# Long convolution and soft MoE on one core: a start without clearings, loads in two bursts per pair of steps, and the signal load split into 64 and 32 rows

## The chip, the core and the metric

The kernel runs on one core of a Trainium2 chip. The metric is the device time in microseconds (us) of one execution, the median of several runs. The engines are PE (TensorE matmul; PEld is its weight load), DVE (VectorE), ACT (ScalarE), POOL (GpSimd) and SP (SyncE, which here only issues DMA transfers). All of them work on their own instruction streams and meet through semaphores.

## The reference

A causal convolution of eight sequences of 5696 tokens and 128 channels with a filter as long as the sequence, and a soft mixture of experts over all 45568 tokens of its output:

```python
# x (8, 5696, 128), h (5696, 128); L = 2 * 5696
y = irfft(rfft(x, L, axis=1) * rfft(h, L, axis=0), L, axis=1)[:, :5696]
x = y.reshape(45568, 128)
logits = x @ phi                         # phi (128, 32): 8 experts, 4 slots each
d = exp(logits - logits.max(0));  d /= d.sum(0) + 1e-9      # over tokens
slot_input = d.T @ x
slot_out[e] = relu(slot_input[e] @ w1[e]) @ w2[e]           # 128 -> 1024 -> 128
c = exp(logits - logits.max(1));  c /= c.sum(1) + 1e-9      # over slots
return c @ slot_out
```

Everything is float32.

## The kernel before

The convolution is done as a transform in two stages, of 90 and 64 points, forward and back, all as matmuls with tables that are loaded from DRAM. Three stages follow each other with a lag, and their intermediates go through DRAM.

- **Stage A** (`stage_a`): the first forward stage. Columns of a sequence are loaded in chunks. `load_x(m)` (line 178) loads one pair of chunks into a tile `xc` of 128 partitions, 4 KB on either side of the sequence to a row; there are two such tiles. The filter `h` has 89 rows and comes as two blocks of 80 and 9 rows; a batch of `x` comes as one block of 96 rows (`XR`). `fold(c)` (209) on POOL adds and subtracts the two sides into one of three tiles `x`; the matmuls at 241 contract all 128 partitions of it. ACT evicts the result into `fst` (243), and SP writes it to DRAM as `f`, low rows (60) in every step, high rows (30) of two chunks in every odd step.
- **Stage B**: `load_g` (264) reads a tile `gt` of `f` (512 KB, 3 buffers). `stage_b1` (275) multiplies by the table `wt` (matmuls at 284) and by the filter's spectrum on DVE (304, 312). For the filter itself (g = 0) it makes that spectrum, `Hr` and `Hi`. `stage_b2` (316) goes back with the table `vt` (327), ACT evicts to `zst` (332), and SP writes `zm` (the first 64 rows) or `zr` (the rest).
- **Stage C**: `load_main` and `load_rest` read `zc` and `zx`, `stage_c1` finishes the transform (412, 417), and c2 to c6 transpose, form logits, both softmaxes, and gather the slots' input. `c_t` keeps the weights in DRAM for the tail, in which the experts and the output are computed.

The steps t = 0, 1, ... of the main loop (631) are written out by hand. A step runs stage A of chunk t, the units of stage B of eight and more steps before, and stage C of a lag of 27 steps. Eight steps (NJ) are one sequence, the filter first and then eight batches; a sequence has 12 units of stage B, one in an odd step and two in an even one. Stage A ends at step 72.

The order in the code is the order on each engine. SP alone issues nearly all transfers, so its instruction order is a queue, too: a transfer that waits holds all behind it. `pending` collects writes, and `flush()` issues them. `prefetch(last)` issues the `gt` loads up to a unit, but none before step 8g + 8 for a sequence g; it is called by `slot_b`, just after `stage_b1` of a unit, so that a load follows each unit (`AHEAD` is 3). In an even step the order of issue is: `load_rest` (only where a batch's first pair needs it), `load_x`, `flush()` of the low `f` writes, and then `gt` after the first unit, writes, `gt` after the second. In an odd step: `flush()`, `load_main`, `load_rest`, `gt`, writes.

Ahead of the loop (615 to 627) SP issues the first two loads of the filter and the tables `wt` and `vt`. ACT issues the other tables and then eight transfers that clear the part of `zr` that stage B never writes; their source is the tile `zx`, cleared by a memset at 359. Memsets at 175 clear the two `xc` tiles, for the rows that no load fills.

Of the kernel before, what the change touches and what calls it, by code (L numbers as in the profile page):

```python
# [70 lines left out]
def kernel(  # L71
# [24 lines left out]
    nc = tc.nc  # L96
    P = 128
# [5 lines left out]
    N1, N2 = 90, 64  # L103
    R1, HALF, NP = S // N2, N2 // 2, N1 // 2
    CH = 4
    NJ = HALF // CH
# [6 lines left out]
    NQ = NJ // 2  # L113
    assert S == R1 * N2 and R1 == N1 - 1 and D == P and CH == Q == 4
    LOW, MAIN = 60, HP
    XR = -(-R1 // 16) * 16
    ctx.enter_context(tc.manual_schedule())

    t_s1, t_im, t_ir, t_w, t_v, t_turn = [
        nc.inline_tensor(t, f"tab_{n}").ap()  # L120
        for n, t in zip(("s1", "im", "ir", "w", "v", "turn"),
                        transform_tables(S, N1, N2, CH, LOW, MAIN, XR))]
# [38 lines left out]
    wt = fconst.tile([P, NP, HP], F32, name="wt")  # L161
    vt = fconst.tile([P, NU, 2, HP], F32, name="vt")
# [9 lines left out]
    xs = {}  # L172
    xf = [apool.tile([P, 2, CH, D], F32, name=f"x{i}", tag=f"x{i}", bufs=1) for i in range(3)]
    xcs = [apool.tile([P, 2, 2 * CH, D], F32, name=f"xc{i}", tag=f"xc{i}", bufs=1) for i in range(2)]
    for t_ in xcs:
        nc.vector.memset(t_[:, :, :, :], 0.0)

    def load_x(m, halves=((0, 2 * CH),)):

        if 2 * m >= (B + 1) * NJ:  # L180
            return
        g, j = divmod(2 * m, NJ)
        if g == 0:
            src, blocks = h, ((0, R1 // 16 * 16), (R1 // 16 * 16, R1))
        else:
            r0 = min((g - 1) * R1, B * R1 - XR) * N2
            src, blocks = x.rearrange("b t d -> (b t) d")[r0:r0 + XR * N2], ((0, XR),)
        src = src.rearrange("(a n) d -> a n d", n=N2)
        t_ = xcs[m % len(xcs)]
        for n0, n in halves:  # L190
            a = (CH * j + n0, N2 - CH * j - n0 - n)
            p = (n0, 2 * CH - n0 - n)
            for r0, r1 in blocks:
                if n == 2 * CH:
                    v = src[r0:r1, a[0]:a[0] + n, :]
                    v = bass.AP(tensor=v.tensor, offset=v.offset,
                                ap=[v.ap[0], [(a[1] - a[0]) * D, 2], [1, n * D]])
                    nc.sync.dma_start(
                        out=t_[r0:r1, :, :, :].rearrange("p s n d -> p s (n d)"), in_=v)
                    continue  # L200
                for s_ in range(2):
                    nc.sync.dma_start(
                        out=t_[r0:r1, s_, p[s_]:p[s_] + n, :].rearrange("p n d -> p (n d)"),
                        in_=src[r0:r1, a[s_]:a[s_] + n, :].rearrange("r n d -> r (n d)"))
        xs[2 * m] = xs[2 * m + 1] = t_

# [2 lines left out]
    def fold(c):  # L209
        if c not in xs:  # L210
            return
        t_ = xs.pop(c)
        y_ = xf[c % len(xf)]
        i = CH * (c % 2)
        near, far = t_[:, 0, i:i + CH, :], t_[:, 1, ::-1, :][:, i:i + CH, :]
        for o in range(2):
            nc.gpsimd.tensor_tensor(out=y_[:, o, :, :], in0=near, in1=far,  # L217
                                    op=AL.subtract if o else AL.add)
        folded[c] = y_

# [2 lines left out]
    def flush():  # L223
        while pending:
            pending.pop(0)()
# [153 lines left out]
    def load_rest(T):  # L379
        if T >= NT:  # L380
            return
        b, j = divmod(T, NQ)
        t_ = zs[T]
        n = 2 * CH
        nc.sync.dma_start(
            out=t_[1][:, :, :, :].rearrange("p h n d -> p (h n d)"),
            in_=zr[(b + 1) % 2].rearrange("o c k r d -> (o c k) r d")[:, j * n:(j + 1) * n].rearrange(
                "p r x -> p (r x)"))
# [212 lines left out]
    NA, NC = (B + 1) * NJ, B * NJ  # L601
# [10 lines left out]
    AHEAD = 3  # L612
# [2 lines left out]
    load_x(0, ((0, CH), (CH, CH)))  # L615
    nc.scalar.dma_start(out=s1[:, :, :, :], in_=t_s1)
    load_x(1)
    nc.sync.dma_start(out=wt[:, :, :], in_=t_w)
    nc.sync.dma_start(out=vt[:, :, :, :], in_=t_v)
    nc.scalar.dma_start(out=phi[:, :], in_=moe_phi)  # L620
    nc.scalar.dma_start(out=turn[:, :, :, :, :], in_=t_turn)
    nc.scalar.dma_start(out=im[:, :, :], in_=t_im)
    nc.scalar.dma_start(out=ir[:, :], in_=t_ir)
    for i in range(8):
        nc.scalar.dma_start(
            out=zr[i // 4][i // 2 % 2, i % 2, N1 - MAIN:].rearrange("k (j r) d -> (k j) (r d)", r=2 * CH),
            in_=zring[0][1][0:4 * (HALF - N1 + MAIN), :, :, :].rearrange("p h n d -> p (h n d)"))
    fold(0)
    wait_b2 = []

    for t in range(last_front + 1):
        us = list(units(t))

        def pair(lag):
            T, half = divmod(t - LAG_C - lag, 2)
            return T if half == 0 and 0 <= T < NT else None

        def prefetch(last):
            nonlocal loaded
            while loaded < len(queue) and queue[loaded][0] <= last \  # L640
                    and queue[loaded][0] // NW * NJ + NJ <= t:
                load_g(queue[loaded][0])
                loaded += 1

        def slot_b(due=True):
            fresh = due and bool(us)
            if fresh:
                u = us.pop(0)
                stage_b1(u)
                prefetch(u + AHEAD)  # L650
                wait_b2.append(u)
            if len(wait_b2) > fresh:
                stage_b2(wait_b2.pop(0))

        T, U, V, W, X = [pair(k) for k in (0, 2, 1, 3, 5)]
        if t < NA:
            stage_a(t, False)
            fold(t + 1)
        if t == last_front:
            assert T is None and U is None  # L660
            assert pair(-1) % NQ
            flush()
            dispatch(W)
            for i in range(3):
                slot_b()
                flush()
                if i == 1:
                    softmax_sum(W)
                    stage_c2(V)
            assert not us and not wait_b2  # L670
            stage_c6(X)
            stage_c3(V)
            column_max(V)
            break
        if t % 2:
            if T is not None:
                stage_c1(T)()
            flush()
            if pair(-2) is not None:
                load_main(pair(-2))  # L680
                if pair(-2) % NQ:
                    load_rest(pair(-2))
            slot_b()
            if U is not None:
                stage_c4(U)
            if t < NA:
                stage_a(t, True)
            if U is not None:
                stage_c5(U)
                softmax_exp(U)  # L690
            flush()
        else:
            if pair(-1) is not None and pair(-1) % NQ == 0:
                load_rest(pair(-1))
            if t < NA:
                load_x(t // 2 + 2)
            flush()
            if t == NJ:
                prefetch(AHEAD - 1)
            slot_b()  # L700
            if W is not None:
                softmax_sum(W)
                dispatch(W)
            flush()
            if V is not None:
                stage_c2(V)
            if X is not None:
                stage_c6(X)
            slot_b()
            if V is not None:  # L710
                stage_c3(V)
                column_max(V)
            flush()
        if t == NA:
            lead.close()
            wts = inner.enter_context(tc.tile_pool(name="wts", bufs=1, side="right"))
            w1s = wts.tile([P, E, F], F32, name="w1s")
        if NA < t <= NA + E:
            nc.sync.dma_start(out=w1s[:, t - NA - 1, :], in_=moe_w1[t - NA - 1])
# [6 lines left out]
    last = work.enter_context(tc.tile_pool(name="last", bufs=1))  # L726
# [8 lines left out]
    y_ = tail["pool"].tile([P, Q * CH, D + 1], F32, name="y2", tag="y2", bufs=1)  # L735
# [6 lines left out]
    for q in range(Q):  # L742
        r = slice(q * NSL, (q + 1) * NSL)
        nc.gpsimd.tensor_copy(out=rep4[r, :, :],
                              in_=ident[r, r].unsqueeze(1).broadcast_to([NSL, Q, NSL]))
# [17 lines left out]
    for V in range(T, NT):  # L763
# [30 lines left out]
        else:  # L794
            for i in range(4 * (V - T - 1), min(4 * (V - T), E), 2):
                nc.sync.dma_start(
                    out=w2s[:, i:i + 2, :, :],
                    in_=moe_w2[i:i + 2].rearrange("e (p c) d -> p e c d", p=P))
# [6 lines left out]
    p = bank()  # L805
# [8 lines left out]
    p = bank()  # L814
# [12 lines left out]
    for g in range(EG):  # L827
        for f0 in range(0, F, FH):
            p = bank()
# [4 lines left out]
            src = p[:, :].rearrange("p (c k) -> p k c", k=NFC)  # L834
# [5 lines left out]
    for g in range(EG):  # L840
        for k0 in range(0, NFC, 4):
            p = bank()
            for k in range(4):
# [3 lines left out]
                out=hidT[:, g, k0:k0 + 4, :], in_=p[:, :].rearrange("p (k c) -> p k c", k=4))  # L847
# [9 lines left out]
    p = bank()  # L857
# [18 lines left out]
    for b in range(B):  # L876
        for w0 in range(0, NV, G4):
            n = min(G4, NV - w0)
# [3 lines left out]
            for k in range(n + lone):  # L882
                for q in range(Q):
                    rows = slice(q * NSL, (q + 1) * NSL)
                    r0 = (w0 + k) * RW
# [3 lines left out]
            for q in range(Q):  # L889
                dst = o_[:, 0:n + lone, q, :]  # L890
                src = pq[q][:, 0:(n + lone) * D].rearrange("p (k d) -> p k d", d=D)
# [41 lines left out]
```

## Time and profile before

| | |
|---|---|
| median of 3 runs | 915.04 us (909.87, 915.04, 915.8) |
| profiled execution, its own time | 909.23 us |
| its span, first to last instruction | 907.4 us |
| mean granted TensorE clock | 0.903 |
| PE busy | 760.2 us, 84% |
| DVE busy | 601.4 us, 66% |
| ACT / POOL busy | 436.8 / 399.8 us |
| DMA moved | 278.33 MB, mean 307 GB/s |

All times of instructions are of that one execution and count from the start of its span. A group line such as `58.85 0.39 SPq L270 DMA_DIRECT2D gt<-f x1` has the start, the duration, the engine or its queue, the line of the kernel, the operation, and output and input by their names. SPq and ACTq are the instructions by which SP and ACT issue transfers. A line `SPq L198 <- DMA zx<-zr: 10.0, 10, 1.7` says that SP waited at line 198 until a transfer of that name had landed, for 10.0 us in total, 10 times, at most 1.7. Writes that go through `flush()` stand at line 225. A line of stretches has the stretch, its length, the busy time of each engine with its number of instructions, the granted clock of PE, the mean busy share of the 16 DMA engines and their rate. That share can pass 1, since the packets of an engine overlap.

### The profile page before, as it was taken

The numbers are of one execution on the slowest core, as the hardware profiler recorded it, in microseconds if no ns is written. First come the engines' busy times: TensorE is split into PE (matmuls) and PEld (weight loads), VectorE is DVE, ScalarE is ACT, GpSimd is POOL, SyncE is SP. The second block draws the span as 40 slices with busy tenths as digits, with TensorE's granted clock in tenths as the row PEclk, the third lists the DMA queues.
The fourth block names the chain that finished last, engine by engine and source line by source line (L and its number), as shares of the span: only waits on it lengthen the run. The fifth ranks groups of instructions, "written<-read, shape, count | busy, mean of one in ns | idle before, by whom it ended". The sixth has DMA issues, their size and how long they took to land.

```text
span 907.4 us, 21291 instructions
## 1 busy us (share of the span) xinstructions
PE 760.2 (84%) x8308; PEld 387.7 (43%) x8308; DVE 601.4 (66%) x896; ACT 436.8 (48%) x880; POOL 399.8 (44%) x353
## 2 busy tenths in 40 slices
PE   6857778689999989999998999799888877767893
PEld 2212233234444444444444444344444434344793
DVE  2029767568778867886877787678778766653552
ACT  2423234335556545665655655456544444563441
POOL 4634322444555655655655566456332224651000
PEclk9979889999999999999999999899988888766855
DMA  8989999999999999999999999999998768540798
GB/s 267 318 275 343 293 296 337 298 314 376 341 291 375 361 326 308 372 358 299 357 364 335 295 373 348 303 308 346 306 291 304 264 200 341 186 166 1 292 406 335
DMA packets 170443, 278.33 MB, mean 307 GB/s; under 512 B 13543, under 2 KB 128231, under 8 KB 165135
## 3 DMA queue, kind: packets, MB, share of 16 engines
q1 hardware_dynamic: 169336, 275.74, 89.7%
q10 hardware_dynamic: 1008, 1.25, 0.5%
q8 instruction: 66, 1.08, 0.5%
q14 instruction: 33, 0.27, 0.1%
HBM read 147.94 MB, written 129.00 MB: 305 GB/s over the span
## 4 chain that ended last, share of the span: by engine, by line
PE 47%; DMA 23%; ACT 8%; POOL 8%; DVE 6%; issue 6%; SPq 1%; ACTq 0%; DVEq 0%; POOLq 0%
PE bank L241 9%; DMA gt<-f 9%; PE bt L284 9%; PE bz L327 6%; POOL y L430 5%; PE bank L412 4%; DMA f<-fst 4%; PE op L886 3%; PE bank L439 3%; PE bank L417 3%; PE bank L448 2%; DMA zx<-zr 2%; ACT fst L243 2%; DMA out_dram<-o 2%; PE bank L527 2%
## 5 line engine op out<-in xcount | busy, mean ns | idle before, releaser
L241 PE MATMUL bank<-x,s 128*32 128x512 f32 (+1 forms) x1152 | 218.0, 620 | 12.9 <-POOL x L217 8.4
L217 POOL TENSOR_TENSOR x<-xc 128x512 f32<-128x512 f32 x144 | 180.4, 1278 | 107.2 <-PE bank L241 86.5
L284 PE MATMUL bt<-gt,wt 64*64 64x256 f32 x1620 | 125.0, 419 | 72.8 <-DMA gt<-f 33.0
L430 POOL TENSOR_TENSOR y<-y,op 128x512 f32<-128x512 f32 x64 | 77.6, 1213 | 206.8 <-DVE op L404 204.3
L304 DVE TENSOR_TENSOR pi<-bt,Hi 128x1024 f32<-128x1024 f32 x96 | 113.0, 1177 | 83.5 <-PE bt L284 83.3
L243 ACT ACTIVATE fst<-bank 128x512 f32<-128x512 f32 x216 | 122.8, 592 | 86.0 <-PE bank L241 57.7
L332 ACT ACTIVATE zst<-bz 128x1024 f32<-128x1024 f32 x96 | 93.3, 972 | 128.3 <-PE bz L327 109.4
L284 PEld LDWEIGHTS bt<-gt,wt 64*64 64x64 f32 x1620 | 58.3, 141 | 151.2 <-issue 79.1
L312 DVE TENSOR_TENSOR yf<-bt,pi 128x512 f32<-128x512 f32 x192 | 119.4, 663 | 3.3
L304 DVE TENSOR_TENSOR bt<-bt,Hr 128x1024 f32<-128x1024 f32 x96 | 113.0, 1177 | 0.0
L241 PEld LDWEIGHTS bank<-x,s 128*32 128x32 f32 (+1 forms) x1152 | 55.1, 126 | 129.8 <-issue 93.6
L327 PE MATMUL bz<-yf,vt 64*64 64x256 f32 x1440 | 110.4, 404 | 0.0
L327 PEld LDWEIGHTS bz<-yf,vt 64*64 64x64 f32 x1440 | 64.3, 143 | 25.5 <-issue 4.2
L512 POOL TENSOR_TENSOR L<-L,rs 128x512 f32<-128x512 f32 x32 | 33.5, 1048 | 91.6 <-DVE rs L511 66.4
L404 DVE TENSOR_TENSOR y<-bank,y 128x512 f32<-128x512 f32 x32 | 22.1, 692 | 76.7 <-ACT y L420 76.5
L439 PE MATMUL bank<-ident,y 109*128 109x109 f32 x512 | 62.7, 273 | 7.9 <-ACT yt L441 7.9
L504 ACT ACTIVATE L<-L 128x512 f32<-128x512 f32 x32 | 20.2, 630 | 94.7 <-POOL L L501 94.6
L430 POOL TENSOR_TENSOR y<-y,om 128x512 f32<-128x512 f32 x54 | 63.9, 1183 | 2.1
L439 PEld LDWEIGHTS bank<-ident,y 109*128 109x128 f32 x512 | 52.9, 149 | 19.4 <-POOL x L217 14.7
L412 PE MATMUL bank<-zc,im 64*64 64x512 f32 x480 | 60.8, 623 | 0.0
L441 ACT ACTIVATE yt<-bank 128x360 f32<-128x360 f32 x128 | 53.0, 482 | 7.7 <-PE bank L439 7.3
L420 ACT ACTIVATE y<-bank 128x512 f32<-128x512 f32 x32 | 19.1, 596 | 72.6 <-PE bank L417 72.6
(101 smaller groups left out, 862.5 us busy)
## 6 DMA issues: line engine op xcount, KB each, us to landing
gt<-f SPq DMA_DIRECT2D x99, 512.0 KB
f<-fst SPq DMA_DIRECT2D x144, 240.0 KB
zm<-zst SPq DMA_DIRECT2D x128, 256.0 KB
zc<-zm SPq DMA_DIRECT2D x30, 1024.0 KB
xc<-in_x_dram SPq DMA_DIRECT2D x32, 768.0 KB
f<-fst SPq DMA_DIRECT2D x144, 120.0 KB
out_dram<-o SPq DMA_DIRECT2D x16, 1024.0 KB
zx<-zr SPq DMA_DIRECT2D x30, 512.0 KB
```

Of the source, the lines that this page charges most:

```text
L217: nc.gpsimd.tensor_tensor(out=y_[:, o, :, :], in0=near, in1=far, op=AL.subtract if o else AL.add)
L241: nc.tensor.matmul(p[i * m:(i + 1) * m, :], s1[:, g // B, q + o, cols], columns(c_, o), start=True, stop=True)
L243: nc.scalar.activation(st[:, :, q, :], p[:, :].rearrange("p (n d) -> p n d", d=D), AF.Copy)
L284: nc.tensor.matmul(bt[q * HP:(q + 1) * HP, a, o, :], wt[r, 2 * i + q, :], t_[r, 2 * o + q, :, :].rearrange("p c d -> p (c d)"), start=True ...
L304: nc.vector.tensor_tensor(out=p_, in0=pv, in1=h_, op=AL.mult)
L312: nc.vector.tensor_tensor(out=y_[r, 0:k, c, :], in0=pv[:, :, c, :], in1=pi[r, 0:k, 1 - c, :], op=op_)
L327: nc.tensor.matmul(bz[a * HP:(a + 1) * HP, q, o, :], vt[r, i, a, :], y_[r, a * m + o, :, :].rearrange("p c d -> p (c d)"), start=True, sto ...
L332: nc.scalar.activation(st[:, 0:m, 0:n, :].rearrange("p o q x -> p q o x"), bz[:, 0:n, 0:m, :], AF.Copy)
L412: nc.tensor.matmul(ps[o, c][h_ * HP:(h_ + 1) * HP, :], im[r, c, :], zt[r, h_, :, c, :], start=True, stop=False)
L430: eng.tensor_tensor(out=part_, in0=part(v, 0), in1=o_[:, :, :], op=sign)
L439: nc.tensor.transpose(p[:, i * TR:(i + 1) * TR], ys[T][0:TR, k * CH + i, 0:D], ident[0:TR, 0:TR])
L441: nc.scalar.activation(yt[:, k * CH:(k + 1) * CH, :, :], of_tokens(p), AF.Copy)
```

## The change

- The memsets of the two `xc` tiles are replaced by memsets of rows 96 to 127 of the three `x` tiles; `fold` reads and writes 96 rows only.
- The filter's load has a third block: rows 82 to 88 once more, into the partitions 89 to 95, which the table multiplies by zero. A batch's load is issued as two transfers: rows 32 to 95, then rows 0 to 31.
- `wt` is loaded in step 3, `vt` in step 9. The eight clearings of `zr` go from ACT's queue ahead of the loop to SP's queue, two in each of the steps 11, 13, 15 and 17.
- The loads stand in two places for a pair of steps. In an even step they follow the first unit's `stage_b1`: `flush()`, `load_rest`, `load_x`, and `refill()`, which issues one `gt`. The second unit of that step is followed by no load. In an odd step `refill()` after `load_main` and `load_rest` issues the `gt` that was left, and another follows the step's unit as before.

```diff
-    for t_ in xcs:
-        nc.vector.memset(t_[:, :, :, :], 0.0)
+    for t_ in xf:
+        nc.vector.memset(t_[XR:P, :, :, :], 0.0)
...
-            src, blocks = h, ((0, R1 // 16 * 16), (R1 // 16 * 16, R1))
+            last = R1 // 16 * 16
+            src, blocks = h, ((0, last, 0), (last, R1, last), (2 * R1 - XR, R1, R1))
         else:
             r0 = min((g - 1) * R1, B * R1 - XR) * N2
-            src, blocks = x.rearrange("b t d -> (b t) d")[r0:r0 + XR * N2], ((0, XR),)
+            src = x.rearrange("b t d -> (b t) d")[r0:r0 + XR * N2]
+            blocks = ((HALF, XR, HALF), (0, HALF, 0))
...
-        near, far = t_[:, 0, i:i + CH, :], t_[:, 1, ::-1, :][:, i:i + CH, :]
+        near, far = t_[0:XR, 0, i:i + CH, :], t_[0:XR, 1, ::-1, :][:, i:i + CH, :]
...
     load_x(1)
-    nc.sync.dma_start(out=wt[:, :, :], in_=t_w)
-    nc.sync.dma_start(out=vt[:, :, :, :], in_=t_v)
...
-    for i in range(8):
-        nc.scalar.dma_start(
+    def clear_rest(i):
+        nc.sync.dma_start(
             out=zr[i // 4][i // 2 % 2, i % 2, N1 - MAIN:].rearrange(...),
             in_=zring[0][1][0:4 * (HALF - N1 + MAIN), :, :, :].rearrange("p h n d -> p (h n d)"))
...
+        def refill():
+            if wait_b2:
+                prefetch(wait_b2[-1] + AHEAD)
+
-        def slot_b(due=True):
+        def slot_b(loads=refill, due=True):
             fresh = due and bool(us)
             if fresh:
                 u = us.pop(0)
                 stage_b1(u)
-                prefetch(u + AHEAD)
                 wait_b2.append(u)
+                loads()
             if len(wait_b2) > fresh:
                 stage_b2(wait_b2.pop(0))
...
         if t % 2:
...
             flush()
+            if t == 3:
+                nc.sync.dma_start(out=wt[:, :, :], in_=t_w)
+            if t == NJ + 1:
+                nc.sync.dma_start(out=vt[:, :, :, :], in_=t_v)
+            if NJ + 2 < t < NJ + 11:
+                clear_rest(t - NJ - 3)
+                clear_rest(t - NJ - 2)
             if pair(-2) is not None:
                 load_main(pair(-2))
                 if pair(-2) % NQ:
                     load_rest(pair(-2))
+            refill()
             slot_b()
...
         else:
-            if pair(-1) is not None and pair(-1) % NQ == 0:
-                load_rest(pair(-1))
-            if t < NA:
-                load_x(t // 2 + 2)
-            flush()
-            if t == NJ:
-                prefetch(AHEAD - 1)
-            slot_b()
+            def burst():
+                flush()
+                if pair(-1) is not None and pair(-1) % NQ == 0:
+                    load_rest(pair(-1))
+                if t < NA:
+                    load_x(t // 2 + 2)
+                if t == NJ:
+                    prefetch(AHEAD - 1)
+                refill()
+
+            if not us:
+                burst()
+            slot_b(burst)
...
-            slot_b()
+            slot_b(lambda: None)
```

## The prediction

> **What bounds the kernel now.** The page first. Its slices show DMA engines near full for three quarters of the span, and TensorE near full only from the second quarter on.
>
> ```profile
> PE   6857778689999989999998999799888877767893
> DMA  8989999999999999999999999999998768540798
> q1 hardware_dynamic: 169336, 275.74, 89.7%
> ```
>
> Then the stretches (length, busy time of PE, PEld, DVE, ACT, POOL, then granted clock, DMA share, GB/s):
>
> ```profile
> 8.40:28.00 19.60, 15.18 (x64) 5.39 (x65) 0.00 (x0) 6.46 (x11) 10.23 (x9) 0.98 0.97 322
> 28.00:49.20 21.20, 18.48 (x80) 5.71 (x80) 0.00 (x0) 10.32 (x19) 15.61 (x13) 0.93 0.97 326
> 58.85:64.95 6.10, 6.10 (x48) 1.79 (x50) 3.65 (x5) 2.39 (x4) 2.82 (x3) 0.78 0.58 165
> 75.74:86.52 10.78, 8.87 (x80) 3.19 (x80) 10.68 (x13) 3.58 (x6) 5.30 (x6) 1.00 1.03 341
> 133.20:149.60 16.40, 13.04 (x130) 5.86 (x130) 10.96 (x12) 6.54 (x9) 4.97 (x4) 0.90 0.99 332
> 369.68:389.83 20.15, 19.39 (x230) 9.35 (x232) 16.07 (x25) 11.87 (x25) 11.76 (x11) 1.00 1.05 364
> 330.00:412.00 82.00, 76.37 (x880) 36.98 (x865) 63.12 (x96) 47.52 (x96) 46.99 (x40) 0.98 1.01 344
> ```
>
> Until 49 us only stage A of the filter runs, and transfers set its pace (share 0.97 at 326 GB/s). From 65 to 97 DVE and DMA are both full; around 61 DMA has a hole (165 GB/s). From 208 to 650, for 5.4 batches, an ordinary pair of steps takes 20.15 us of which TensorE works 19.39 at full clock, so four pairs cannot take less than 80.6 us; the batches take 82.0 to 83.0, mean 82.3. The missing 1.7 us sits where a batch begins: TensorE waits there for `gt`, and the chain of waits shows `DMA gt<-f` at 9.4%.
>
> Third, the start (start, duration, engine, line):
>
> ```profile
> 1.23 1.76 DVE L176 MEMSET xc<- 128x2048 f32 x1 [1.23 <-PEq L919]
> 3.02 3.71 SPq L202 DMA_DIRECT2D xc<-in_h_dram  x8
> 6.24 6.53 ACTq L625 DMA_DIRECT2D zr<-zx  x8
> 7.04 4.92 POOL L217 TENSOR_TENSOR x<-xc 128x512 f32<-128x512 f32 x4 [5.71 <-DMA xc<-in_h_dram]
> 12.80 1.28 ACT L243 ACT_TABLE_LOAD   x1 [12.80 <-DMA zr<-zx]
> ```
>
> The first load waits for the first clearing, and ACT cannot evict before 14.09 because it issues eight clearings of `zr` until 12.77. Last, the queue of SP in steady state, which says who waits in front of what:
>
> ```profile
> SPq L225 <- DMA gt<-f: 42.1, 50, 2.4
> SPq L198 <- DMA zx<-zr: 10.0, 10, 1.7
> 291.63 0.69 SPq L270 DMA_DIRECT2D gt<-f  x1
> 297.86 0.43 SPq L270 DMA_DIRECT2D gt<-f  x1
> ```
>
> `zx` stands eight transfers ahead of `xc` in SP's order, and the other releasers fit too: a transfer is issued once the one eight places ahead has landed. So SP runs some 6 us behind its data, and the order of the queue is the order of service.
>
> **The start, part by part.** The `xc` memsets (2 x 1.76 us) give way to three of 1024 elements on 32 partitions; the `zx` clearing of 1024 elements took 0.91, so 2.7 us, on a DVE that is then idle until 58.85. They no longer stand ahead of the load: issue moves from 3.02 to about 0.7, where ACT's first transfer is issued. Against that the filter's load has three blocks of rows instead of two, so six issues instead of four ahead of the first fold, at 3.71/8 = 0.46 us: 0.9 us. First fold at 7.04 - 2.3 + 0.9 = 5.7.
>
> The eight `zr` clearings leave ACT, its table load goes to about 4, and the first eviction is bounded by TensorE instead: some 2 us earlier. But DMA then has too little to do from about 8.5 to 13 (only the third filter load, 0.73 MB or 2.2 us), which eats the 2.3 us that the load gained. Counted at nothing together.
>
> What counts is bytes. `vt` (1.51 MB) and the clearings (8 x 96 KB, 0.79 MB) leave the DMA-limited stretch ahead of the first `gt`; `wt`, moved to step 3, stays in it. 2.29 MB at 326 GB/s is 7.0 us; I take 6.8, as the first 3 us were not full. So the first stage B matmul goes from 56.80 to 50.
>
> They come back later. `vt` is issued in step 9, behind the low `f` writes and ahead of the `gt` of unit 3; the hole at 58.85 to 64.95 takes 6.1 x (330 - 165) = 1.0 MB. The other 1.29 MB, two clearings to an odd step included (on SP, ahead of the `gt` loads there), meet the stretch to 107 at 309 to 347 GB/s. Steady state reached 373 in one window, so absorbed for nothing at best; at 330 GB/s 3.9 us. DVE hides it, with 10.68 of 10.78 us busy, and late `gt` tiles show at once. I take 1.5. **Start: -5.3, between -8 and 0.**
>
> **The x load.** The rates in 0.25 us slices from 284 us, around the issue of `xc` at 285.84:
>
> ```profile
> GB/s 393 381 393 397 361 365 360 356 385 397 422 397 320 369 336 369 393 344 360 360 279 279 246 246 234 221 266 410 385 422 361 377 397 377 397 348 373 372 363 368
> ```
>
> For seven slices, from 289.0 to 290.75, the rate is 253 instead of 375. That is 1.75 x (1 - 253/375) = 0.57 us lost per pair. At the start of a batch, with the queue empty, the same dip follows the `xc` issue, so it is the load and not the `f` writes behind it. The split gains between 0.57 (dip gone) and -0.34 (one more issue, if SP were the limit; it isn't while it waits for landings). I take 0.2 per pair, 0.8 per batch.
>
> The Trainium skill, DMA: Bandwidth & Descriptors, Rules for kernel authors, speaks against the split: transfers to disjoint partition halves serialise on the same 16 engines, so use one. By that rule this term is 0 or a small loss. SBUF — State Buffer, Door 1, puts partitions 0 to 63 on eight ports and 64 to 127 on the other eight: 96 rows load one set twice as much, which agrees with a dip; rows 32 to 95 load both evenly, rows 0 to 31 one set only, so by its 218 GB/s for eight ports an estimate of 1.4 + 1.2 = 2.6 us for the two transfers, little better than one.
>
> **The bursts.** In an even step the order `load_rest`, `xc`, `f` writes, first `gt`, ... second `gt` becomes `f` writes, `load_rest`, `xc` twice, first `gt`. Once per batch `load_rest` waits on SP for landing `zr` writes (5.6 us over 8 times); `f` now passes it, up to 0.7 per batch, hidden while older transfers are queued: 0.
>
> The second `gt` moves to the next odd step, past two `zm` writes, two `f` writes, `zc` and `zx`. Its tile is needed one pair later: it was issued at 291.63 and that unit's matmuls ran at 303.34. The next `gt`, issued at 297.86 behind `zc` and `zx`, freed its place only at 307.55, when the `f` write eight places behind it went out: 9.7 us. Moved there, the second `gt` goes out near 296.4 (its own 0.52 MB, 1.4 us at 364 GB/s, no longer ahead of `zc`) and lands near 306.1: 2.8 us late. Behind it on TensorE wait that b1, the b2 after it, c3 and the next low stage A; behind these `f` and `zc`. One such stall shortens the 6 us backlog, and the next tile is on time; the stall at the batch's start then shrinks, as its `gt` meets the shorter queue too. So between +2.8 per batch (nothing shrinks) and -1.7 (the 80.6 us floor). I take 0: where both TensorE and DMA are this full, a stall only moves. **Steady: 0.8 x 5.4 = -4.3, between -9.2 and +15.**
>
> After 650 stage A has ended and DMA share is 0.87 to 0.90; the tail is untouched.
>
> **Sum.** The profiled execution took 909.23 (span 907.4). 909.2 - 5.3 - 4.3 = 899.6. It was the quickest of four: the others are 909.87, 915.04 and 915.8, mean of four 912.5, 3.3 above it. So 903 for the median to be measured, 1.3% below 915.04. No change can be told from one of about 1%.
>
> **Rivals.**
> - *The floor* (0.18): bursts and split free DMA enough that all batches run at 80.6: 909.2 - 5.3 - 9.2 + 3.3 = 898; with the start's best -8, 895. For it: ordinary pairs already run at 20.15 exactly. Against: the batch's first pair holds sixteen small `zr` writes at 300 GB/s.
> - *Bytes are conserved* (0.16): DMA is full from 3 to 650, what leaves the start returns by 107, the split serialises: 909 to 912. For it: 0.97 and 1.03 shares on both sides. Against: the hole at 61.
> - *The late `gt`* (0.20), slower: the second `gt` is 2.8 us late once per batch without paying back at the batch's start: +15 with the start's gain gives 909.2 - 5.3 + 15 + 3.3 = 922, without it 927. It decides as soon as that tile lands after its unit's old start, 303.34 in the pair shown, in every batch anew. Repeated in all 16 ordinary pairs it would be +45. Against: the stall drains the queue that causes it.
> - *The split does nothing* falls inside my own case: 907 with the 3.3.
>
> **Chances.** My case 0.46, own range 895 to 912; about two thirds of it lies below 906. Faster: 0.30 + 0.18 = 0.48; same: 0.16 + 0.16 = 0.32; slower 0.20. The range runs from the floor with an uncommonly good start (886) to between the late-`gt` prices (924).
>
> **Right or wrong.** Right: first fold near 5.7, first stage B matmul near 50, first stage B of the signal (105.16 before) near 100; steady batches of 81 to 82; the dip in GB/s shallower; second `gt` issued after `zx`, with a stall `PE bt L284 <- DMA gt<-f` no longer than before in total (13.1 us from 190 to 660). Wrong: that wait grows beyond 20 us or appears in ordinary pairs; pairs of more than 20.15 us between batch starts; or the first 107 us as long as before.

## Result and profile after: slower by 3.6%

The changed kernel takes 947.87 us in the median of 4 runs (942.89 to 951.78), the kernel before 915.42 in 4 runs beside it (909.87 to 919.68). The ratio is 1.0355, with a 95% interval of 1.0281 to 1.0429. The profiled execution took 947.49 us, its span 945.4 at a mean granted clock of 0.888; before it was 909.23, 907.4 and 0.903. The prediction was 903 and faster.

The page of the changed kernel, the slices of PE and DMA and the queue:

```profile
PE   6857687788988998997999899988978877767893
DMA  6999979999999999999999999999988867460698
q1 hardware_dynamic: 170248, 276.76, 88.6%
```

Nearly as many bytes are moved as before (276.76 MB in this queue, 275.74 before); both are a little less full for longer. In the chain that ended last, the share of `DMA gt<-f` has gone from 9% to 16%:

```profile
DMA gt<-f 16%; PE bank L244 9%; PE bt L287 8%; DMA zm<-zst 5%; PE bz L330 5%; PE bank L415 3%; DMA out_dram<-o 3%; PE bank L420 2%; DMA f<-fst 2%; SPq L228 2%; PE bank L451 2%; PE bank L442 2%; PE op L904 2%; DMA zx<-zr 2%; PE bank L530 2%
```

Where the 38.0 us of the two spans lie is read from the first and the last instruction of a kind: the first matmuls of stage C (line 412 before, 415 after) start at 203.9 instead of 185.9, the last ones of stage A at 686.2 instead of 647.9, and from there to the end it is 259.2 instead of 259.5. So 18.0 us are lost before stage C begins, 20.3 in the 5.4 batches after it, and nothing in the tail. Not all of this is waiting. The same 8308 matmuls keep TensorE busy for 777.3 us instead of 760.2, at a lower granted clock; 12.1 us of that lie before stage C and 5.0 in the batches. The last section comes back to this.

The stretches of the changed kernel: the start, an ordinary pair of steps, the pair in which a batch begins, and a whole batch (length, busy PE, PEld, DVE, ACT, POOL, then clock, DMA share, GB/s):

```profile
0.00:28.00 28.00, 19.02 (x78) 6.11 (x79) 4.78 (x9) 9.64 (x15) 15.62 (x19) 1.00 0.73 194
28.00:49.20 21.20, 15.69 (x70) 3.69 (x66) 0.00 (x0) 7.92 (x14) 10.09 (x9) 1.00 0.94 323
...
107.00:133.00 26.00, 17.18 (x118) 6.35 (x118) 13.67 (x19) 5.63 (x8) 4.96 (x4) 0.70 0.89 251
...
224.28:244.06 19.78, 19.02 (x227) 8.98 (x225) 15.88 (x24) 11.40 (x22) 11.75 (x10) 1.00 1.00 348
263.76:286.64 22.88, 20.43 (x219) 9.62 (x217) 15.23 (x22) 11.85 (x24) 11.65 (x10) 0.93 0.92 278
222.50:310.00 87.50, 80.43 (x886) 37.89 (x886) 62.88 (x96) 47.27 (x95) 44.76 (x39) 0.94 0.97 318
```

The ordinary pair is as short as before (19.78 us; before, such pairs took 19.7 to 20.2), but the batch takes 87.5 instead of 82.0. The loss is not spread: it sits where a batch begins. The waits of PE from 190 to 660 us, of the changed kernel (total, times, longest):

```profile
PE bt L287 <- DMA gt<-f: 23.0, 10, 5.3
...
PE bank L420 <- DMA zx<-zr: 6.9, 4, 3.1
```

and of the kernel before:

```profile
PE bt L284 <- DMA gt<-f: 13.1, 5, 5.5
...
PE bank L417 <- DMA zx<-zr: 2.5, 2, 2.3
```

Before there was one `gt` stall to a batch; now there are two, and one for `zx` in most batches. One of these can be followed. SP's queue around a batch's start in the changed kernel (start, duration, line, transfer, number):

```profile
279.09 6.48 SPq L228 DMA_DIRECT2D f<-fst  x6
285.67 0.58 SPq L388 DMA_DIRECT2D zx<-zr  x1
286.29 1.32 SPq L201 DMA_DIRECT2D xc<-in_x_dram  x2
287.71 0.38 SPq L273 DMA_DIRECT2D gt<-f  x1
```

and TensorE at the same place:

```profile
286.64 1.95 PE L415 MATMUL bank<-zc,im 64*64 64x512 f32 x16
291.69 2.02 PE L420 MATMUL bank<-zx,ir 26*64 26x512 f32 x16 [3.10 <-DMA zx<-zr]
```

Four high and two low `f` writes go ahead of `zx`. It is issued only 1 us before the stage C that needs it begins, and the second half of that waits 3.10 us. At these six writes SP waits for the landing of older loads, and for no eviction (279 to 286.5 us):

```profile
SPq L228 <- DMA gt<-f: 2.2, 2, 1.1
SPq L228 <- DMA zc<-zm: 0.9, 1, 0.9
```

In the tables below "pair A" is the pair of steps, from one start of stage C's matmuls to the next, in which a batch's first units of stage B run (0 to 2); "pair B" is the one after it, with units 3 to 5 and the first `zx` of the batch. Each is the mean over the five batches of one profiled execution. The other pairs stayed at 19.9 on average (20.1 to 20.2 where the whole burst order stood).

### The profile page after: what moved, and what is told of

Read it like the earlier page. It is cut to its first block, busy times and chain, and to the rows that moved or that the text cites. A ratio compares the mean times of both kernels' runs of the same rounds, so it can differ in the third digit from the quotient of the medians.

```text
span 945.4 us, 21295 instructions
## 1 busy us (share of the span) xinstructions
PE 777.3 (82%) x8308; PEld 391.7 (41%) x8308; DVE 601.3 (64%) x897; ACT 438.6 (46%) x880; POOL 399.4 (42%) x353
## 3 DMA queue, kind: packets, MB, share of 16 engines
q1 hardware_dynamic: 170248, 276.76, 88.6%
## 4 chain that ended last, share of the span: by engine, by line
PE 40%; DMA 34%; DVE 8%; issue 5%; SPq 4%; ACT 4%; POOL 4%; DVEq 0%; ACTq 0%; POOLq 0%
DMA gt<-f 16%; PE bank L244 9%; PE bt L287 8%; DMA zm<-zst 5%; PE bz L330 5%; PE bank L415 3%; DMA out_dram<-o 3%; PE bank L420 2%; DMA f<-fst 2%; SPq L228 2%; PE bank L451 2%; PE bank L442 2%; PE op L904 2%; DMA zx<-zr 2%; PE bank L530 2%
## 5 line engine op out<-in xcount | busy, mean ns | idle before, releaser
L244 PE MATMUL bank<-x,s 128*32 128x512 f32 (+1 forms) x1152 | 228.4, 643 | 13.5 <-POOL x L220 13.4
L220 POOL TENSOR_TENSOR x<-xc 96x512 f32<-96x512 f32 x144 | 180.0, 1274 | 123.5 <-PE bank L244 101.1
L287 PE MATMUL bt<-gt,wt 64*64 64x256 f32 x1620 | 127.9, 426 | 89.8 <-DMA gt<-f 51.9
L330 PE MATMUL bz<-yf,vt 64*64 64x256 f32 x1440 | 112.7, 408 | 0.0
L330 PEld LDWEIGHTS bz<-yf,vt 64*64 64x64 f32 x1440 | 65.8, 144 | 24.9 <-issue 4.3
L407 DVE TENSOR_TENSOR y<-bank,y 128x512 f32<-128x512 f32 x32 | 22.1, 692 | 83.2 <-ACT y L423 82.9
L507 ACT ACTIVATE L<-L 128x512 f32<-128x512 f32 x32 | 20.2, 630 | 88.1 <-POOL L L504 88.1
L423 ACT ACTIVATE y<-bank 128x512 f32<-128x512 f32 x32 | 19.1, 596 | 78.0 <-PE bank L420 78.0
```

Of the source, the lines that this page charges most:

```text
L220: nc.gpsimd.tensor_tensor(out=y_[0:XR, o, :, :], in0=near, in1=far, op=AL.subtract if o else AL.add)
L244: nc.tensor.matmul(p[i * m:(i + 1) * m, :], s1[:, g // B, q + o, cols], columns(c_, o), start=True, stop=True)
L287: nc.tensor.matmul(bt[q * HP:(q + 1) * HP, a, o, :], wt[r, 2 * i + q, :], t_[r, 2 * o + q, :, :].rearrange("p c d -> p (c d)"), start=True ...
L330: nc.tensor.matmul(bz[a * HP:(a + 1) * HP, q, o, :], vt[r, i, a, :], y_[r, a * m + o, :, :].rearrange("p c d -> p (c d)"), start=True, sto ...
```

## Experiments: the parts of the change

Ratios are to the kernel before, run beside each kernel on the same chip, with 95% intervals.

**The split alone** (`split_only`).

```diff
-            src, blocks = x.rearrange("b t d -> (b t) d")[r0:r0 + XR * N2], ((0, XR),)
+            src, blocks = x.rearrange("b t d -> (b t) d")[r0:r0 + XR * N2], ((HALF, XR), (0, HALF))
```

> The kernel before with only the signal load issued as rows 32 to 95 and rows 0 to 31; clearings, tables and load order as before. Theory split (the two transfers take about 1.1 us more per pair of steps than one, in each of the 32 pairs that load a batch): 945 to 952. Theory late gt and theory start (the split is neutral): 908 to 919, and the batches stay at 82 to 83 us.

Measured: 924.43 us, 1.0121 (1.0085 to 1.0157), between the ranges of the theories.

**The order alone** (`bursts_only`): the kernel before with `refill`, `burst` and `slot_b(loads)` of the changed one.

> The kernel before with only the new order of the loads. Theory split: 908 to 919. Theory late gt (the second gt of a pair is late and the delay is not paid back): 930 to 940, with a wait of TensorE for gt from stage B of the first batch to the end of stage A of above 20 us against 13.1 before. Theory start: 908 to 919.

Measured: 946.63 us, 1.0338 (1.0292 to 1.0384).

**The start alone** (`start_only`): the changed kernel with the order and the single transfer of before.

> The kernel before with only the new start: memsets on 32 rows, wt in step 3, vt in step 9, the clearings of zr in steps 11 to 17, filler rows in the filter's load. My forecast's term: 5 us below before, 905 to 912. Theory start (vt and wt arrive in front of what stage B needs, and cost what they saved and more): 920 to 928, stage B of the signal beginning near 114 instead of 105. Theory split: like the forecast's term.

Measured: 914.46 us, 1.0002 (0.9969 to 1.0036).

**The change without the split** (`whole_x`).

```diff
-            blocks = ((HALF, XR, HALF), (0, HALF, 0))
+            blocks = ((0, XR, 0),)
```

> The changed kernel with the signal load as one transfer of 96 rows again. Theory split: 905 to 918. Theory late gt or start: 940 to 950, as the changed kernel. If two parts share the blame, in between, and the difference to the changed kernel is the split's share in company.

Measured: 946.83 us, 1.0349 (1.0311 to 1.0387).

**The change without the order** (`order_of_before`): the new start and the split, loads where they stood before.

> The changed kernel with the loads where they were before: the new start and the split remain. If parts add: 914 + 11 = 920 to 930. If the split costs nothing beside the new start: 910 to 918.

Measured: 921.92 us, 1.0084 (1.006 to 1.0107).

What follows: the new order makes nearly all of the loss, alone or with the rest. The start is worth nothing at the end. The split costs about 1% under the old order and nothing that can be told under the new one, so the parts do not add up.

## Experiments: which move of the order

**The low `f` writes ahead of `load_rest` and `load_x`, nothing else** (`swap_only`).

```diff
+            flush()
             if pair(-1) is not None and pair(-1) % NQ == 0:
                 load_rest(pair(-1))
             if t < NA:
                 load_x(t // 2 + 2)
-            flush()
```

> The kernel before with one change: in an even step the two low f writes are issued ahead of load_rest and load_x instead of behind them. Theory one direction (runs of f writes, four high and then two low with no load between, move at about 200 GB/s, and that costs some 1.1 us in every one of the 36 pairs, from the filter's stage A on): 935 to 948, with the first gt matmul near 61. Theory late gt: this is free, 906 to 918, first gt matmul near 57.

Measured: 935.63 us, 1.0268 (1.0199 to 1.0338). This lies in the range of the first theory, but its reason does not hold: the ordinary pairs stay at 19.9 us, and by themselves the transfers run as fast in that order (354 GB/s against 353, below).

**The second `gt` of an even step moved behind `zc` and `zx` of the next odd step, nothing else** (`second_gt_only`): `burst` with `load_rest` and `load_x` ahead of `flush()`.

```diff
+            refill()          # odd step, behind load_main and load_rest
...
-            slot_b()          # second unit of an even step
+            slot_b(lambda: None)
```

> The kernel before with only the second gt of a pair moved behind zc and zx of the next odd step, and the first left where it was; load_x stays ahead of the f writes. Theory late gt: 930 to 948, with waits of TensorE for gt in ordinary pairs. Theory one direction: 908 to 922, the first 57 us as before.

Measured: 931.32 us, 1.0223 (1.0163 to 1.0284).

**The same `gt` moved, but ahead of `zc` and `zx`** (`second_gt_ahead_of_zc`).

```diff
+            refill()
             if pair(-2) is not None:
                 load_main(pair(-2))
                 if pair(-2) % NQ:
                     load_rest(pair(-2))
-            refill()
```

> Like the kernel with only the second gt moved, but in the odd step it goes out ahead of zc and zx instead of behind them. The run of loads is the same four, and the tile lands about 4.4 us earlier (1.57 MB at 360 GB/s). Theory late gt: 908 to 920. Theory one direction: 926 to 936, as with the gt behind zc.

Measured: 919.09 us, 1.007 (1.0032 to 1.0107). So about two thirds of this move's cost is `zc` and `zx` in front of it.

The trace of `second_gt_only` shows the place. SP's queue, where `gt` goes behind `zx`:

```profile
283.04 0.34 SPq L385 DMA_DIRECT2D zx<-zr  x1
283.64 1.16 SPq L270 DMA_DIRECT2D gt<-f  x2
```

and TensorE, which waits for the tile:

```profile
293.52 1.76 PE L284 MATMUL bt<-gt,wt 64*64 64x256 f32 x16 [3.27 <-DMA gt<-f]
```

The two moves differ in what they make late. Waits of PE from 208 to 690, first `second_gt_only`, then `swap_only`:

```profile
PE bt L284 <- DMA gt<-f: 22.5, 10, 3.7
```

```profile
PE bt L284 <- DMA gt<-f: 17.0, 4, 5.7
...
PE bank L417 <- DMA zx<-zr: 7.1, 4, 2.8
```

**Which of the two that `f` passes matters.** Two kernels move the low `f` writes past one of them each. The first:

```diff
                 load_rest(pair(-1))
+            flush()
             if t < NA:
                 load_x(t // 2 + 2)
-            flush()
```

> The kernel before with the low f writes ahead of the x load in every even step, but behind the zx load that a batch's first pair needs. Theory 1 (the place of zx is what costs): x has a pair of time to spare, so 0 to +0.5%, 915 to 920 us, and no wait for zx beyond the 2.7 us of before. Theory 2 (x behind f closes a loop over fold, stage A and f, and the place of x costs): +1.5 to 2.7%, 929 to 940 us, with the pairs of a batch's start longer and no zx wait.

Measured: 930.72 us, 1.0192 (1.0155 to 1.023).

The second has `load_x`, `flush()`, `load_rest` in this order.

> The kernel before with the zx load that a batch's first pair needs behind x and the low f writes (order x, f, zx). Theory 1 (zx late): TensorE waits for zx once per batch as where f passed both (7.1 us in all there), +1.5 to 2.7%, 929 to 940 us. Theory 2 (the place of x costs): 0 to +0.5%, 915 to 920 us. If both runs of this pair stay below +1%, the cost is of the two together.

Measured: 924.34 us, 1.0136 (1.0089 to 1.0184).

Neither theory alone was right: both cost. The waits again, `f_ahead_of_x` and then `f_ahead_of_zx`, each have one kind only:

```profile
PE bt L284 <- DMA gt<-f: 24.2, 6, 6.8
```

```profile
PE bank L417 <- DMA zx<-zr: 20.6, 5, 4.8
...
PE bt L284 <- DMA gt<-f: 2.6, 3, 1.3
```

With `zx` late the `gt` stall of before nearly goes, and with `x` late it grows. Why a late `x` makes the first `gt` late was not tried by itself. The loop `x`, fold, stage A, `f` write, `gt` is the likely way, and that is argued only.

**Half-way** (`f_interleaved`): the `x` load between the two low `f` writes in the even step, `load_main` between them in the odd one.

```diff
+            if pending:
+                pending.pop(0)()
             if t < NA:
                 load_x(t // 2 + 2)
             flush()
```

> The kernel before with the two low f writes of a step taken apart: in an even step load_x stands between them, in an odd step load_main does. Theory one direction: 896 to 910, batches nearer the 80.6 us floor and the first gt matmul at 54 to 57. Theory late gt has no opinion: 908 to 918. If a write that waits in front of a load costs more than the mixing gains: 918 to 930.

Measured: 914.71 us, 1.0037 (1.0004 to 1.007). One write instead of two in front of `x` costs little, and a better mix brings nothing (in the transfers alone, below, `x` between its writes makes 304 GB/s, ahead of them 317).

The pairs, from one profiled execution each (us, and what A and B together exceed 2 x 20.15 by):

| kernel | pair A | pair B | excess per batch | ratio |
|---|---|---|---|---|
| before | 22.6 | 20.2 | 2.6 | 1 |
| split_only | 25.2 | 20.2 | 5.1 | 1.012 |
| f_ahead_of_x | 26.0 | 20.1 | 5.8 | 1.019 |
| f_ahead_of_zx | 20.2 | 25.2 | 5.0 | 1.014 |
| swap_only | 24.9 | 21.6 | 6.2 | 1.027 |
| second_gt_only | 21.1 | 24.9 | 5.7 | 1.022 |
| second_gt_ahead_of_zc | 25.0 | 20.4 | 5.1 | 1.007 |
| bursts_only | 23.5 | 24.6 | 7.8 | 1.034 |
| after | 24.0 | 22.8 | 6.5 | 1.036 |

A delay of `x` shows in A, a delay of `zx`, or of the second `gt` behind it, in B. With the second `gt` ahead of `zc` the long pair is A; that profiled execution, 926.68 us, was the slowest of ten, and why the stall sits there stays open. One stall does shrink the other (20.2 and 21.1 in A where B is long), but never by as much as it costs. Multiplied by 5.4 batches, `second_gt_only` has (5.7 - 2.6) x 5.4 = 17 of the 21.3 us between the two profiled spans (928.7 and 907.4) in these pairs, and `bursts_only` 28 of 43.3; another 13.3 of the latter were lost before stage C (first matmuls at 199.2 against 185.9).

## Experiments: the transfers by themselves

**Transfers without computation** (`transfers_alone`): SP issues each kind of transfer, and then each order of a whole pair, with no data to wait for.

> No computation: only transfers of the kernel's shapes from SP, one kind after the other, with nothing that any of them waits for but the queue, then the repeating orders of a pair of steps: as before, with f ahead of x, with the second gt late, with both, and as changed. Its output is not the reference's. Theory one direction (the order alone sets the rate): the order of before runs near 19.5 us a pair, the one with f ahead of x and the one with the second gt late 1 us or more longer, both 1.5 or more; x as 64 and 32 rows no faster than one transfer. Theory waiting (late data hold the queue up and the rate only follows): all four orders within 0.3 us of each other.

Measured, the middle of each phase (the last two numbers are DMA share and GB/s). In this order: `x` as 96 rows, `x` as 64 and 32, `x` by sides, low `f`, high `f`, `x` ahead of a pair's `f` writes, `x` between them, `gt`, `zm`, then pairs in the order of before, with `f` ahead, with the second `gt` late, with both, and as changed with the split:

```profile
15.00:50.00 35.00, 0.00 (x0) 0.00 (x0) 1.00 1.03 253
75.00:138.00 63.00, 0.00 (x0) 0.00 (x0) 1.00 1.03 256
155.00:210.00 55.00, 0.00 (x0) 0.00 (x0) 1.00 1.03 263
225.00:250.00 25.00, 0.00 (x0) 0.00 (x0) 1.00 0.96 388
260.00:296.00 36.00, 0.00 (x0) 0.00 (x0) 1.00 0.86 259
310.00:383.00 73.00, 0.00 (x0) 0.00 (x0) 1.00 0.95 317
395.00:470.00 75.00, 0.00 (x0) 0.00 (x0) 1.00 0.93 304
482.00:515.00 33.00, 0.00 (x0) 0.00 (x0) 1.00 1.10 349
528.00:567.00 39.00, 0.00 (x0) 0.00 (x0) 1.00 1.05 360
590.00:728.00 138.00, 0.00 (x0) 0.00 (x0) 1.00 1.03 353
750.00:890.00 140.00, 0.00 (x0) 0.00 (x0) 1.00 1.03 354
910.00:1050.00 140.00, 0.00 (x0) 0.00 (x0) 1.00 1.03 358
1075.00:1214.00 139.00, 0.00 (x0) 0.00 (x0) 1.00 1.03 352
1235.00:1377.00 142.00, 0.00 (x0) 0.00 (x0) 1.00 1.02 349
```

Two things follow. The order does not change what DMA moves per second (349 to 358 in all five, which are orders of an ordinary pair, in one run). And a pair of steps holds 7.16 MB (`x` 768 KB, four `f` writes of 240 and four of 120, three `gt` of 512, six `zm` of 256, `zc` 1024, `zx` 512, `c_t` 180): at 353 GB/s that is 20.3 us, while TensorE's ordinary pair takes 20.15. The two are about equal (at the 364 GB/s of one ordinary pair before it would be 19.7 us). And TensorE makes nothing up: in the kernels of the table all but `bursts_only` and the changed one have ordinary pairs of 19.9 to 20.0 us on average, whether a long pair goes before or not. That both being full is the reason is argued.

**`x` as two transfers of 96 rows** (`x_by_sides`), one for each side of the sequence: two issues, but none with fewer partitions.

```diff
-                if n == 2 * CH:
+                if n == 2 * CH and g == 0:
```

> The kernel before with the signal load issued as two transfers of all 96 rows, one for each side of the sequence: as many transfers and bytes as the split by rows, but the rows as before. If the split's 1.2% comes from one more transfer in a queue eight deep: 920 to 930. If it comes from the shape of 64 and 32 rows: 908 to 918.

Measured: 918.69 us, 1.0073 (1.0041 to 1.0106), against 1.0121 for rows. So being two transfers costs by itself. Whether the split by rows costs more than that stays open, as the intervals overlap.

## Experiments: is the stall at a batch's start a matter of place?

The kernel before waits 13.1 us for a batch's first `gt`. The next kernels move that load; `early` lets `prefetch` go one step sooner.

```diff
             if U is not None:
                 stage_c5(U)
                 softmax_exp(U)
             flush()
+            if t % NJ == NJ - 1 and t > NJ:
+                prefetch(t // NJ * NW, 1)
```

> The kernel before with only the first gt of each batch moved: it is issued at the end of the odd step before, behind that step's high f writes and ahead of zx, x and the next low f writes, instead of behind them. In the trace of before the pair that holds this unit is on average 2.6 us longer than 20.15 (23.8, 22.6, 20.5, 26.2, 20.4). Theory 1 (the stall at a batch's start comes from the place of this load in SP's order): it shrinks to at most 1 us, -5 to -13 us, 902 to 910 us, unless SP has to wait for f to land in front of it. Theory 2 (transfers have no reserve there, so a load that goes earlier makes another later): within 0.5%, 911 to 919 us, and the wait moves to zx or to the next gt. Slower than 925 us if SP stands in front of that load until the high f writes have landed.

Measured: 916.5 us, 1.0025 (0.9998 to 1.0053).

In the second, a `flush()` and the two added lines stand ahead of the step's high stage A instead.

> As the run with the first gt behind the high f writes, but ahead of them, so that only the low f writes of two matmul groups earlier must have landed. Theory 1: -5 to -13 us, 902 to 910 us, the better of the two if SP must wait for f to land. Theory 2: within 0.5% of before, 911 to 919 us. If SP waits here for the low f writes to land, the high f writes and zx behind it go out later by that wait, and a stall of that length appears at zx: +1 to +2%.

Measured: 910.36 us, 0.9942 (0.9906 to 0.9978). The waits of PE in it, from 208 to 690, have no `gt` in their first lines any more:

```profile
PE bank L417 <- DMA zx<-zr: 14.2, 5, 4.3
PE bank L439 <- ACT yt L441: 8.5, 18, 0.5
PE bt L284 <- DVE yf L312: 7.4, 18, 0.7
```

The `gt` stall of 13.1 us is gone, and a `zx` stall of 14.2 stands in the next pair (A 20.2, B 23.7). A load that goes earlier makes another later. What was won lies ahead of stage C, where there is no `zx`: its first matmuls start at 182.8 instead of 185.9.

So the third keeps the early load for the two batches before stage C (`if t in (2 * NJ - 1, 3 * NJ - 1)`), and the fourth adds the new start.

> The kernel before with the first gt issued behind the high f writes of the odd step before, in the first two batches only. Theory 1 (the early load gains where no zx load competes, and trades places with zx elsewhere): the first stage C comes at 179 to 183 us instead of 185.9, all later batches are as before, so -3 to -7 us, 906 to 911 us, ratio 0.992 to 0.997. Theory 2 (what is gained there is lost again, as the start's gain was): first stage C earlier but the first steady batch longer by as much, ratio 0.998 to 1.002.

Measured: 908.99 us, 0.9956 (0.9924 to 0.9988); stage C starts at 182.3.

> The same early load in the first two batches, on the kernel with the new start (no clearings of xc, three blocks of the filter, wt and vt and the clearings of zr later). Theory 1 (the start's 1.4 us were lost in the stalls of the first two batches): another -1 to -2 us beside early_gt_without_zx. Theory 2 (what the start leaves out comes back as transfers before 107 us): the same time as early_gt_without_zx within 0.2%.

Measured: 909.3 us, 0.9965 (0.9933 to 0.9997); stage C starts at 178.5 in the profile, but the medians of the two are equal. `first_gt_before_high_f` and `early_gt_without_zx` are faster than the kernel before by about half a per cent; which of them is better can't be told.

## Why the prediction was wrong, point by point

- **Bursts, `f` ahead of the loads: "up to 0.7 per batch, hidden while older transfers are queued: 0".** This step failed first. It costs +2.7% alone (`swap_only`). I asked what the wait at `load_rest` delays, and not what `f` delays: `zx` and `x` then stand behind two more writes of 240 KB. Each of the two costs by itself (+1.4 and +1.9%).
- **Bursts, the second `gt`: "2.8 us late", once per batch.** Place and mechanism were right: it was issued behind `zx`, and the stall of 3.27 us shown above is close to the 2.8. But it was priced at its length alone. In the mean of five batches pair B grew by 4.7, and 1.6 of that are not idle: TensorE is busy for 21.0 us in it instead of 19.4, with the same matmuls. Alone it costs +2.2%, 20 us, where the rival of the late `gt` had +15.
- **"I take 0: where both TensorE and DMA are this full, a stall only moves."** This is the choice that decided the number, and it was wrong. The pair at the batch's start did shrink, from 22.6 to 21.1 in `second_gt_only`, but by 1.5 against 4.7. That both are full speaks against making up lost time: the transfers of a pair alone take 20.3 us, about as long as the pair. The bound of +2.8 per batch was also too low: `bursts_only` has 7.8 - 2.6 = 5.2, as a batch then has two stalls. The floor of 80.6 us was none either: in the kernel before the four pairs from 247.4 us take 80.2. And the lower end of 886 does not follow from its terms, which give 895.
- **The x load: 0.2 gained per pair.** Measured +1.2% by itself, some 11 us; the term's bound for a loss, 0.34 per pair, is 0.34 x 4 x 5.4 = 7. The dip in the trace was a trait of the load, as I said, but 253 GB/s alone and 256 when split show that the split does not remove it. In the changed kernel the dip is longer, not shallower: nine slices of 0.25 us at 111 to 246 GB/s from 291.5 (the rates below begin at 286.5), where before there were seven at 253. That is at a batch's start, but an ordinary pair has it too: after the issue at 330.53 us the rate falls to 66 GB/s.

```profile
GB/s 164 246 393 311 246 213 229 279 279 328 344 360 262 328 262 295 311 295 254 299 229 188 246 184 160 111 193 160 242 340 328 340 344 373 388 377 385 369 402 397
```

  The Trainium skill, DMA: Bandwidth & Descriptors, Rules for kernel authors, says not to split a transfer into disjoint partition halves, since they share the same engines; the runs agree that it gains nothing (253 against 256 GB/s), and here it costs (1.0121). SBUF — State Buffer, Door 1, gave the estimate of 2.6 us for the two transfers; 768 KB at 256 GB/s is 3.07 us, so the measurement does not show the gain that an even load of the ports would bring.
- **The start: -5.3, first fold at 5.7, first stage B matmul at 50.** They came at 7.51 and 58.89 in the changed kernel, 55.4 with the start alone. The queue's first transfers tell why the first fold was late:

```profile
0.73 1.62 SPq L205 DMA_DIRECT2D xc<-in_h_dram  x4
5.20 3.08 SPq L205 DMA_DIRECT2D xc<-in_h_dram  x8
```

  The first four issues took 0.41 us each, no more than counted. But then SP waited 2.8 us until one of them had landed, and the third block, which the first fold needs, went out only at 5.20. Four transfers of ACT were out by then, too; whether they count towards the eight was not tried. And bytes were not what counted. Without `vt` and the clearings in the way, DMA idles: from 0 to 28 us it moves 194 GB/s at a share of 0.73 (with the start alone 229 at 0.80; before, 276 at 0.88), so the bytes taken out left a hole instead of time. With the start alone, the `gt` loads were issued 2.8 us earlier and the first unit ran 1.4 us earlier; by the first stage C, at 185.9 in both, nothing was left. The rival that bytes are conserved named this outcome, but by another way: it has DMA full, and DMA had holes.
- **Signs of right and wrong.** The `gt` wait passed the 20 us that I had named as wrong (23.0), and the first 107 us were not shorter: the signal's stage B began at 116.28 instead of 105.16. Ordinary pairs stayed nearly without a stall, as I expected (20.2 us on average). The rival of the late `gt` named the sign and one of the two causes; its 922 or 927 lacks the `f` writes' part and the slower matmuls behind a wait.

## What to carry to other kernels

Where the slowest engine and the transfers need the same time for a unit of work, each new stall stays in the total, and the cheapest assumption, that it moves, has to be worked out by asking where the slack is. A stall of TensorE is to be priced at more than its length: look at the matmuls behind it, too. When a queue's order changes, price what is passed as well as what passes: list for each transfer now standing later when it is needed and what its new predecessors wait for. A transfer moved earlier in a full queue takes its place from another one; look for a stretch where that other one does not exist.

## What the runs showed of the hardware

- The same engines move 388 GB/s for 60-row writes of 240 KB, 349 for `gt`, 253 for the 96-row `x` load, and 259 at a share of only 0.86 for 30-row writes of 120 KB. Rates are a matter of shape, so bytes alone do not price a transfer.
- A wait of TensorE costs more than its own length. In `f_ahead_of_x` it waits 6.78 us for a `gt`, until 435.06; the granted clock (the third number from the end) falls during the wait, to 0.50, and has nearly returned at 440 to 444:

```profile
424.00:428.00 4.00, 4.00 (x40) 1.06 (x36) 1.44 (x4) 1.46 (x4) 1.55 (x2) 1.00 0.85 260
428.00:432.00 4.00, 0.28 (x8) 0.00 (x0) 2.67 (x4) 1.09 (x2) 0.94 (x1) 0.77 0.99 269
432.00:436.00 4.00, 0.94 (x12) 0.67 (x16) 0.00 (x0) 0.00 (x0) 3.72 (x4) 0.50 1.07 303
436.00:440.00 4.00, 4.00 (x28) 1.85 (x24) 2.86 (x3) 1.42 (x4) 0.00 (x0) 0.50 1.12 365
440.00:444.00 4.00, 4.00 (x28) 1.12 (x24) 1.38 (x3) 3.03 (x8) 2.54 (x3) 0.95 1.03 355
```

  It is so throughout. The profiles of the 18 kernels that compute have 90 pairs A. In the 30 of at most 21 us TensorE is busy for 18.8 to 19.1 us, in the 58 of 22.3 us and more for 20.4 to 22.0; the two between, of 21.4 and 22.1, have 19.0 and 18.9. The slower matmuls stand behind the wait: in the changed kernel's `zx` stall, shown above, 16 matmuls take 2.02 us that took 1.11 before.
- The same shows ahead of stage C. In the changed kernel the granted clock is 0.70 from 107 to 133 us, against 0.89 before over the same stretch, and stage A's matmuls took 728 ns on average from 107 to 208 instead of 631 (two shapes together).
